# Batch 0 of an FFT convolution with an MLP behind it: stage A by pairs of columns, its output pushed into stage B's layout, the first D block kept on chip, weight conversions spread, tiles at multiples of 64 bytes

## The chip, the cores and the metric

One core of a Trainium2 chip runs the whole program. Its engines are TensorE (PE in the profile; PEld is its weight load), VectorE (DVE), ScalarE (ACT), GpSimd (POOL) and SyncE (SP), which here only issues transfers. The metric is the device time of one execution in microseconds; a comparison uses the median of several runs.

## What is computed

The input `x` is 8 batches of 3072 positions by 256 channels. Each channel is filtered along the positions in the frequency domain, and the result goes through a two-layer MLP with a softplus between.

```python
X = np.fft.rfft(x, axis=1)                       # (8, 3072, 256)
F = (filt_r + 1j * filt_i)[None, :, :]
y = np.fft.irfft(X * F, n=x.shape[1], axis=1)
h = y.reshape(-1, 256) @ w_in                    # 256 -> 2048
g = np.maximum(h, 0.0) + np.log1p(np.exp(-np.abs(h)))
out = g @ w_out                                  # 2048 -> 256
```

The weights arrive in float64 and are turned into float32 pairs on the chip.

## The kernel before

**Numbers.** Nearly every operand of a matmul is split into a rounded part and the rest (`hi_lo`, called `inh`/`inl`, `zh`/`zl`, `dih`/`dil`, `gh`/`gl` in the profile), and `split_mm` (line 67) makes three products of them. So each operand costs one cast and one subtraction before PE can use it.

**The transform** of 3072 = 128 x 12 x 2 positions goes in four stages per batch. *A*: for each of the 12 columns `i`, the two halves of `x` are added (even `i`) or subtracted (odd `i`), split, and multiplied by a 128x128 matrix `ca`; the output is `s1`. *B*: 13 units `u` of 120 rows (ten frequencies by twelve columns; the last has 96) are multiplied by `cb`; DVE multiplies the result with the filter rows `ft` in three instructions (lines 185, 186, 189), POOL adds the two halves (line 190). *C*: the inverse of B; the output `co` goes to DRAM as `s2`. *D*: for each of six blocks of 512 positions a last product, and the sums `y` that become the MLP's input `yT` (hi and lo).

Between A and B the layout changes: A's rows are frequencies, B's rows are (frequency, column). Later batches write A's output to DRAM and read it back in B's layout. Batch 0 keeps it on chip in `first_s1`, and each unit copies its part from ten partitions to 120 with two transfers on SP (line 153, `bi`), followed by two filter loads (lines 163 and 164, `ft`), through three rotating buffers each.

**The MLP** runs in 48 groups of 512 positions, 8 steps each. A step is `mm1` (12 products into `h`), ACT's Abs, Exp and Ln, then `soft` on DVE (the softplus row, line 298, the cast `gh`, line 300, the rest `gl`, line 302) and, two steps later, `mm2` (12 products into `o`). `h` has two buffers, so `mm1` of step s+2 waits for the softplus row of step s.

**Weights.** Each of 16 weight tiles is loaded with 512 KB (line 334) and converted by six DVE rows (`weight`, lines 348 to 361), then a cast on ACT and two POOL rows (`weight_ends`, lines 375 to 377). Tiles 0 to 7 belong to `w_in`: 2j and 2j+1 are needed by steps 2j and 2j+1. Tiles 8 to 15 belong to `w_out`: tile 8+s is needed by `mm2` of step s. `together` converts two tiles row by row in turn.

**What sets the order.** It is written by hand (`manual_schedule`): each engine executes its instructions in the order in which the Python code issues them. Batch 0 runs first, alone, through a table of visits (`first`); then the loop over steps interleaves the MLP of one batch with stages A to D of the next by a table of slots. Of the weights, 0, 1, 2 are converted in A and between A and B, 3 in the first unit of B, 8, 9, 4 between C and D, 5 and 11 behind D's first block, and the other seven one per step in `soft`:

```python
CONVERSIONS = {("a", 9): (0,), ("a", 11): (1, 2), ("b", 0): (3,), ("c", 12): (8, 9, 4)}
WEIGHTS = (5, 11), (10,), (6,), (7,), (12,), (13,), (14,), (15,)
```

An engine that waits holds all that is queued behind it. A transfer issued on SP or ACT also waits in that engine's order.

Of the kernel before, what the change touches and what calls it, by code (L numbers as in the profile page):

```python
# [25 lines left out]
F32 = mybir.dt.float32  # L26
# [8 lines left out]
NU = 13  # L35
# [3 lines left out]
LOADS = {("a", 8): (0,), ("a", 10): (2, 3), ("c", 9): (9,), ("c", 11): (8, 4), ("d", 1): (11,), ("y", 0): (5,)}  # L39
CONVERSIONS = {("a", 9): (0,), ("a", 11): (1, 2), ("b", 0): (3,), ("c", 12): (8, 9, 4)}  # L40
WEIGHTS = (5, 11), (10,), (6,), (7,), (12,), (13,), (14,), (15,)
TAGS = {1: "in", 2: "ca", 4: "in", 5: "in", 8: "in", 11: "ca"}
# [5 lines left out]
def fft_mlp(ctx: ExitStack, tc: tile.TileContext, x, fr, fi, ca, cb, cc, cd, w_in, w_out, out):  # L48
# [13 lines left out]
    wi = [const.tile([P, 2, FF], F32R, name=f"wi{k}") for k in range(2)]  # L62

# [19 lines left out]
    class Batch:  # L83
# [5 lines left out]
        def engines(self, first):  # L89

            return (nc.vector, nc.gpsimd) if self.b or first else (nc.scalar, nc.vector)

        def a_load(self, i):
            if i == 0 and self.b:
                self.s1 = dram.tile([2, P, N2, D], F32, tag="s1", name="s1")
            if self.b or i < 6:
                xt = work.tile([P, 2, 512], F32, tag="in", name="x", bufs=3)
            else:
                xt = start.tile([P, 2, 512], F32, name=f"x{i}")
# [4 lines left out]
            cat = (work if self.b or i >= 8 else start).tile(  # L104
                [P, 2, 2, 2, P], F32R, tag="ca" if self.b or i >= 8 else f"ca{i}", name="ca", bufs=2 if self.b or i >= 8 else 1
            )
# [11 lines left out]
        def a_prep(self, i):  # L118
            if self.b or i == 0:
                self.a_sum(i)  # L120
            st = self.t.pop(("as", i))
            if self.b == 0 and i + 1 < N2:
                self.a_sum(i + 1)
            self.t["ap", i] = hi_lo(st, P, "in", *self.engines(0))

        def a_mm(self, i):
# [7 lines left out]
            if self.b == 0:  # L134
                nc.scalar.activation(out=first_s1[i % 2][:, n2:n2 + 2].rearrange("p n d -> p (n d)"), in_=ps, func=AF.Copy)
                return
# [11 lines left out]
        def b_load(self, u):  # L148
            p = self.filled(u)
            bt = work.tile([P, 512], F32, tag="bi", name="bi", bufs=3)  # L150
            if self.b == 0:
                for h in range(2):
                    nc.sync.dma_start(
                        out=bt[:p, 256 * h:256 * h + 256],
                        in_=first_s1[h][10 * u:10 * u + p // N2],
                    )
# [308 lines left out]
    with tc.manual_schedule():  # L465
        nc.scalar.preload_act_table_set("natural_log_exp_and_others")
        def first(part):
            for q in part:
                p = seq[q][1:]
                run.ahead(q)  # L470
                if p == ("c", 2):
                    batches[0].e_load(0)
# [160 lines left out]
```

## Time and profile before

| what | value |
|---|---|
| runs | 2553.85, 2555.40, 2555.42 us; median 2555.4 |
| profiled execution | 2552.4 us, of which the span from first to last instruction is 2550.6 |
| mean granted TensorE clock | 0.975 |
| busy over the span | PE 2452.6 us (96%), DVE 2049.8 (80%), ACT 1494.8 (59%), POOL 747.3 (29%) |
| first product of A / of B / of D / of the MLP | 8.02 / 36.40 / 123.42 / 131.62 us |
| last copy of A begins; last row of C on ACT begins | 31.09; 113.72 us |
| softplus rows of steps 0 and 7 begin | 141.96 and 202.05 us |

All times are from the span's start. PE's share of 96% is an average: it is full for most of the program, and the places where it isn't are in the first 203 us. A busy time counts an instruction from its start to its end, and neighbours on one engine overlap a little, so for a chain of instructions the distance from start to start is the better price. What ended a wait stands in a row in brackets, or in the table of waits behind the arrow.

### The profile page before, as it was taken

The numbers are of one execution on the slowest core, as the hardware profiler recorded it, in microseconds if no ns is written. First come the engines' busy times: TensorE is split into PE (matmuls) and PEld (weight loads), VectorE is DVE, ScalarE is ACT, GpSimd is POOL, SyncE is SP. The second block draws the span as 40 slices with busy tenths as digits, with TensorE's granted clock in tenths as the row PEclk, the third lists the DMA queues.
The fourth block names the chain that finished last, engine by engine and source line by source line (L and its number), as shares of the span: only waits on it lengthen the run. The fifth ranks groups of instructions, "written<-read, shape, count | busy, mean of one in ns | idle before, by whom it ended". The sixth has DMA issues, their size and how long they took to land.

```text
span 2550.6 us, 31103 instructions
## 1 busy us (share of the span) xinstructions
PE 2452.6 (96%) x11232; PEld 2027.6 (79%) x11232; DVE 2049.8 (80%) x2575; ACT 1494.8 (59%) x1742; POOL 747.3 (29%) x610
## 2 busy tenths in 40 slices
PE   4589999999999999999999999999999999999999
PEld 3267777888888888888888888888888888888887
DVE  7799896889868898789878888688887899766665
ACT  3355655566656666666665666665665666665555
POOL 3544331333213332233313333143221433111110
PEclk7589999999999999999999999999999999999999
DMA  7724432343324341243323433233422533111100
GB/s 206 194 87 147 128 99 81 121 127 86 86 86 132 118 112 54 85 163 104 89 61 125 134 95 83 90 124 104 118 71 71 170 105 93 44 42 34 42 17 17
DMA packets 145673, 251.38 MB, mean 99 GB/s; under 512 B 12849, under 2 KB 63345, under 8 KB 145521
## 3 DMA queue, kind: packets, MB, share of 16 engines
q1 hardware_dynamic: 93168, 151.36, 19.4%
q0 software_dynamic: 14112, 50.86, 6.7%
q10 hardware_dynamic: 38240, 47.20, 6.3%
q8 instruction: 88, 1.44, 0.2%
q14 instruction: 65, 0.52, 0.1%
HBM read 173.87 MB, written 72.35 MB: 97 GB/s over the span
## 4 chain that ended last, share of the span: by engine, by line
PE 88%; DVE 6%; DMA 2%; issue 1%; ACT 1%; SPq 1%; POOL 0%; ACTq 0%; DVEq 0%; POOLq 0%
PE h L67 39%; PE o L67 39%; PE psd L245 3%; PE psa L67 2%; PE psb L67 2%; PE psc L67 2%; DMA bi<-s 1%; DVE s L298 1%; DMA x<-in_x 1%; DVE gl L302 0%; DVE gh L300 0%; DMA s<-co 0%; SPq L164 0%; DVE t L186 0%; DVE inh L73 0%
## 5 line engine op out<-in xcount | busy, mean ns | idle before, releaser
L67 PE MATMUL h<-yT,wi 128*128 128x512 f32 x4608 | 1117.9, 392 | 13.2 <-DVE s L298 11.6
L67 PEld LDWEIGHTS h<-yT,wi 128*128 128x128 f32 x4608 | 859.2, 189 | 190.1 <-DVE s L298 10.6
L67 PE MATMUL o<-gh,wo 128*128 128x512 f32 x3072 | 952.0, 391 | 5.6 <-ACT ob L325 5.2
L289 ACT ACTIVATE s<-h 128x1024 f32<-128x1024 f32 x384 | 395.0, 1029 | 717.1 <-PE h L67 678.3
L67 PEld LDWEIGHTS o<-gh,wo 128*128 128x128 f32 x3072 | 569.0, 189 | 118.1 <-ACT ob L325 5.9
L298 DVE SCALAR_TENSOR_TENSOR s<-h,s 128x1024 f32<-128x1024 f32 x384 | 467.9, 1219 | 178.2 <-ACT s L291 176.5
L67 PE MATMUL o<-gl,wo 128*128 128x512 f32 x1536 | 599.4, 390 | 3.7 <-DVE gl L302 3.7
L302 DVE TENSOR_TENSOR gl<-s,gh 128x1024 fp32r<-128x1024 f32 x384 | 471.4, 1228 | 36.5 <-DVE gh L300 0.9
L290 ACT ACTIVATE s<-s 128x1024 f32<-128x1024 f32 x384 | 407.8, 1062 | 12.2
L291 ACT ACTIVATE s<-s 128x1024 f32<-128x1024 f32 x384 | 407.7, 1062 | 12.2
L300 DVE CAST gh<-s 128x1024 fp32r<-128x1024 f32 x384 | 315.3, 821 | 36.6 <-DVE s L298 2.3
L67 PEld LDWEIGHTS o<-gl,wo 128*128 128x128 f32 x1536 | 289.0, 188 | 67.0 <-DVE gl L302 6.0
L271 POOL TENSOR_TENSOR yT<-y,yT 128x512 fp32r<-128x512 f32 x94 | 126.2, 1343 | 605.6 <-DVE yT L73 605.6
L190 POOL TENSOR_TENSOR t<-t,t 128x512 f32<-128x512 f32 x104 | 147.9, 1422 | 401.7 <-DVE t L189 295.5
L79 POOL TENSOR_TENSOR inl<-bi,inh 128x512 fp32r<-128x512 f32 (+2 forms) x100 | 132.4, 1324 | 293.3 <-issue 104.6
L79 POOL TENSOR_TENSOR dil<-di,dih 128x512 fp32r<-128x512 f32 x94 | 121.6, 1294 | 208.4 <-DVE dih L73 140.3
L257 DVE TENSOR_TENSOR sd<-psd,ev 128x256 f32<-128x256 f32 x192 | 80.6, 420 | 117.1 <-ACT ev L256 117.0
L79 POOL TENSOR_TENSOR inl<-st,inh 128x512 fp32r<-128x512 f32 x84 | 118.1, 1405 | 168.2 <-DVE inh L73 163.9
L79 DVE TENSOR_TENSOR zl<-t,zh 128x512 fp32r<-128x512 f32 x104 | 90.5, 870 | 56.3 <-ACT zh L71 54.0
L245 PE MATMUL psd<-cd,dih 128*128 128x256 f32 x384 | 100.9, 285 | 11.7 <-ACT dih L71 9.7
L245 PE MATMUL psd<-cd,dil 128*128 128x256 f32 x384 | 101.8, 286 | 3.0 <-DVE dil L79 3.0
L67 PE MATMUL psb<-inh,cb_sb 128*128 128x512 f32 (+3 forms) x224 | 73.0, 411 | 23.8 <-ACT inh L71 22.6
(60 smaller groups left out, 1806.9 us busy)
## 6 DMA issues: line engine op xcount, KB each, us to landing
ft<-in_fr SPq DMA_DIRECT2D x104, 256.0 KB
x<-in_x SPq DMA_DIRECT2D x48, 512.0 KB
ca<-in_ca POOLq DMA_DIRECT2D x48, 512.0 KB, 4.8
cd<-in_cd POOLq DMA_DIRECT2D x48, 512.0 KB, 4.0
di<-s SPq DMA_DIRECT2D x96, 256.0 KB
out<-ob SPq DMA_DIRECT2D x48, 512.0 KB
s<-co ACTq DMA_DIRECT2D x96, 240.0 KB
s<-ao ACTq DMA_DIRECT2D x84, 256.0 KB
```

Of the source, the lines that this page charges most:

```text
L67: nc.tensor.matmul(out=ps, lhsT=lhs[a], rhs=rhs[b], start=first and k == 0, stop=last and k == 2)
L79: lo_eng.tensor_sub(out=lo[:p], in0=src, in1=hi[:p].bitcast(F32))
L190: nc.gpsimd.tensor_add(out=t1, in0=t1, in1=t2)
L245: nc.tensor.matmul(out=ps[:, h].rearrange("p k n -> p (k n)"), lhsT=ds[k][:, h, 128 * c:128 * c + 128], rhs=cdt[:, h, j].rearrange("p k n ...
L257: nc.vector.tensor_add(out=s[:, j], in0=ps[:, :, 0], in1=ev)
L271: lo_eng.tensor_sub(out=lo[:, c], in0=y, in1=hi[:, c].bitcast(F32))
L289: nc.scalar.activation(out=a, in_=h, func=AF.Abs)
L290: nc.scalar.activation(out=a, in_=a, func=AF.Exp, scale=-1.0)
L291: nc.scalar.activation(out=a, in_=a, func=AF.Ln, bias=1.0)
L298: nc.vector.scalar_tensor_tensor(out=a, in0=h, scalar=0.0, in1=a, op0=ALU.max, op1=ALU.add)
L300: nc.vector.tensor_copy(out=hi, in_=a)
L302: nc.vector.tensor_sub(out=lo, in0=a, in1=hi.bitcast(F32))
```

## The change

Batch 0 gets code of its own, and the table of visits for it goes.

**A** (`first_a`) works by pairs of columns: one tile holds both halves' sum and difference, one ACT pass makes both casts, one DVE row both rests, 24 matmuls fill one two-bank accumulator, one ACT pass takes it out. The matrix `ca0` has its output columns reordered, so that a transfer can carry each column's rows straight into B's layout `s1b`: twelve pushes (`shuffle`), each of a 120-row and an 8-row transfer, alternately on SP and ACT. The pushes of pairs 0 and 1 are issued with pair 2.

**B and C** (`first_bc`) read `s1b` in place. All 26 filter loads are issued ahead on SP into tiles of their own, then the loads of weights 2, 8, 3, 4. Weights 0 and 1 are converted before B's first unit. The rests `inl` are made by DVE for units 0, 1, 2 and odd ones, else by POOL (before: by DVE for 0, 2, 3, 7). Each output of C, besides going to DRAM, is copied by two small transfers on SP into the first D block's input `di`, so D's load from DRAM falls away for that block.

**D** (`first_d`): weights 8 and 2 are converted before it, weight 3 in pieces between its rows. Weights 4 to 7 and 9 to 15 are left to the first eight steps, up to two per step. In those steps the cast `gh` is ACT's, and the second D block's casts are ACT's too. New pools lie at the right end of the memory, with each tile of theirs at a multiple of 64 bytes. The arithmetic is the same: PE has 10818 rows in either program, and from B's first unit on they are the same rows in the same order.

SP, where stages B and C of batch 0 end. Before (`s_82`, `s_83` are the two halves of A's output; `s_427` is `s2`):

```order
L153 DMA bi<-s_82 96x1x256
L153 DMA bi<-s_83 96x1x256
L163 DMA ft<-in_fr 128x512
L164 DMA ft<-in_fi 64x512
L334 DMA raw<-in_w_out 128x1024 x2
L334 DMA raw<-in_w_in 128x1024
L226 DMA di<-s_427 128x512 x2
```

and now (`raw` is a weight's tile):

```order
L466 DMA fr_315<-in_fr 128x512
L467 DMA fi_311<-in_fi 64x512
L466 DMA fr_319<-in_fr 128x512
L467 DMA fi_318<-in_fi 64x512
L327 DMA raw<-in_w_in 128x1024
L327 DMA raw<-in_w_out 128x1024
L327 DMA raw<-in_w_in 128x1024 x2
L203 DMA di<-co 10x2x256 x24
L203 DMA di<-co 8x2x256 x2
```

The copies `bi` are gone, the load of `di` from DRAM too, and the copies from `co` stand behind all filters and weights.

DVE, from stage A into B's first units. Now (`lo` is A's rest, lines 341 to 354 are a conversion, lines 170 to 174 the products with the filter):

```order
L520 TENSOR_TENSOR lo<-st,hi 128x1024 x2
L341 TENSOR_SCALAR m<-raw 128x512
L342 TENSOR_SCALAR p<-raw 128x512
L341 TENSOR_SCALAR m<-raw 128x512
L342 TENSOR_SCALAR p<-raw 128x512
L346 SCALAR_TENSOR_TENSOR raw<-raw,p 128x512 x2
L350 SCALAR_TENSOR_TENSOR raw<-m,raw 128x512 x2
L352 TENSOR_SCALAR p<-raw 128x512 x2
L354 SCALAR_TENSOR_TENSOR raw<-raw,p 128x512 x2
L79 TENSOR_TENSOR inl<-s1b,inh 120x512 x2
L170 TENSOR_TENSOR t_370<-psb,fr_273 128x512
```

Before, DVE's conversions of weights 0, 1 and 2 stood among A's last columns and behind them, and that of weight 3 behind the products of B's first unit; now both conversions stand between A's last row and B's first.

DVE, from the softplus row of one early step to the next. Before:

```order
L298 SCALAR_TENSOR_TENSOR s<-h,s 128x1024
L348 TENSOR_SCALAR m<-raw 128x512
L349 TENSOR_SCALAR p<-raw 128x512
L300 CAST gh<-s 128x1024
L353 SCALAR_TENSOR_TENSOR raw<-raw,p 128x512
L302 TENSOR_TENSOR gl<-s,gh 128x1024
L357 SCALAR_TENSOR_TENSOR raw<-m,raw 128x512
L359 TENSOR_SCALAR p<-raw 128x512
L361 SCALAR_TENSOR_TENSOR raw<-raw,p 128x512
```

and now, in the step with weights 5 and 9:

```order
L291 SCALAR_TENSOR_TENSOR s<-h,s 128x1024
L341 TENSOR_SCALAR m<-raw 128x512
L342 TENSOR_SCALAR p<-raw 128x512
L346 SCALAR_TENSOR_TENSOR raw<-raw,p 128x512
L295 TENSOR_TENSOR gl<-s,gh 128x1024
L350 SCALAR_TENSOR_TENSOR raw<-m,raw 128x512
L352 TENSOR_SCALAR p<-raw 128x512
L354 SCALAR_TENSOR_TENSOR raw<-raw,p 128x512
L341 TENSOR_SCALAR m<-raw 128x512
L342 TENSOR_SCALAR p<-raw 128x512
L346 SCALAR_TENSOR_TENSOR raw<-raw,p 128x512
L350 SCALAR_TENSOR_TENSOR raw<-m,raw 128x512
```

The cast `gh` has left DVE, and a second conversion stands behind the first.

The core of the diff:

```diff
+WEIGHTS = (4,), (5, 9), (10, 6), (7, 11), (12,), (13,), (14,), (15,)
...
-        def engines(self, first):
-            return (nc.vector, nc.gpsimd) if self.b or first else (nc.scalar, nc.vector)
+        def engines(self, blk):
+            if self.b or blk > 1:
+                return nc.vector, nc.gpsimd
+            return nc.scalar, nc.gpsimd if blk else nc.vector
...
-            if self.b == 0:
-                for h in range(2):
-                    nc.sync.dma_start(
-                        out=bt[:p, 256 * h:256 * h + 256],
-                        in_=first_s1[h][10 * u:10 * u + p // N2],
-                    )
...
-            self.t["bp", u] = hi_lo(self.t["b", u][0][:p], p, "in", hi_eng, lo_eng if u in (0, 2, 3, 7) else nc.gpsimd)
+            self.t["bp", u] = hi_lo(src[:p], p, "in", hi_eng, lo_eng if u < 3 or u % 2 else nc.gpsimd)
...
+            if self.b == 0:
+                dt = self.t["d", 0][0]
+                for n in range(2):
+                    nc.sync.dma_start(
+                        out=dt[10 * u:10 * u + p // N2, :, n],
+                        in_=co[:p].rearrange("(r n) (h d) -> n r h d", n=N2, h=2)[n],
+                    )
...
-        nc.vector.tensor_copy(out=hi, in_=a)
+        copy(nc.scalar if s < len(WEIGHTS) else nc.vector, hi, a)
...
+    def filter_load(v, pool):
+        fit = pool.tile([P, 512], F32, name=f"fi{v}", align_bytes=64)
...
+            nc.sync.dma_start(out=frt, in_=fr[u])
+            nc.sync.dma_start(out=half, in_=fi[u])
...
+    def first_a(s1_b, start):
...
+        def sums(p):
+            xt = xts.pop(p)
+            st = sts[p] = start.tile([P, 2, 512], F32, tag="st", name="st", align_bytes=64)
+            nc.vector.tensor_add(out=st[:, 0], in0=xt[:, 0], in1=xt[:, 1])
+            nc.vector.tensor_sub(out=st[:, 1], in0=xt[:, 0], in1=xt[:, 1])
+            his[p] = start.tile([P, 2, 512], F32R, tag="hi", name="hi", align_bytes=64)
+            nc.scalar.activation(out=his[p], in_=st, func=AF.Copy)
+
+        def shuffle(p):
+            ao = aos.pop(p)
+            for j in range(2):
+                eng = (nc.sync, nc.scalar)[j]
+                for q, rows, u in ((slice(0, 120), 120, slice(0, NU - 1)), (slice(120, P), 96, slice(NU - 1, NU))):
+                    eng.dma_start(
+                        out=s1_b[:rows, u].rearrange("(r n) u c -> n r u c", n=N2)[2 * p + j],
+                        in_=ao[q, j],
+                    )
...
+            if p >= 2:
+                shuffle(p)
+            if 3 <= p < 5:
+                weight_load(p - 3)
+
+    def first_bc(s1_b, filters, pool):
...
+        for k in (2, 8, 3, 4):
+            weight_load(k)
+        together((0, 1))
+        weight_ends()
+        bt.e_load(0)
+        bt.t["d", 0] = work.tile([P, 2, 2, D], F32, tag="di", name="di"), bt.t.pop(("e", 0))
+        bt.b_prep(0)
+        for i in range(NU + 2):
+            if i + 1 < NU:
+                bt.b_prep(i + 1)
+            if i < NU:
+                bt.b_mm(i)
+            if 0 < i <= NU:
+                bt.z_mm(i - 1)
+            if i >= 2:
+                bt.c_mm(i - 2)
...
+    def first_d():
+        together((8, 2))
+        weight_ends()
+        more = weight(3)
+        bt.d_prep(0)
+        bt.d_prep(1)
+        for _, k, i in d_visits(0):
+            getattr(bt, f"{k}_mm")(i)
+            next(more, None)
...
-                soft(s, chain(*(weight(k) for k in (WEIGHTS[s + 1] if s + 1 < len(WEIGHTS) else ()))))
+                soft(s, chain(*(weight(k) for k in (WEIGHTS[s] if s < len(WEIGHTS) else ()))))
...
+    order = [10 * u + r for r in range(10) for u in range(NU - 1)] + list(range(120, 128))
```

More of the change, by code (lines that the diff above doesn't have):

```diff
@@ L62, in fft_mlp @@
     wi = [const.tile([P, 2, FF], F32R, name=f"wi{k}") for k in range(2)]
+    other = dict(side="right", reuse_waits="tile")
     def split_mm(ps, lhs, rhs, first=True, last=True):
@@ L465, in fft_mlp @@
+    def first_d():
[7 more added lines that the diff above has]
+            next(more, None)
+        for _ in more:
+            pass
+        weight_ends()
     with tc.manual_schedule():
         nc.scalar.preload_act_table_set("natural_log_exp_and_others")
[L467 to L472, printed above, removed]
-                run.do(q)
-                for k in LOADS.get(p, ()):
-                    weight_load(k)
-                together(CONVERSIONS.get(p, ()))
-                weight_ends()
@@ L479, in fft_mlp @@
-        seq = visits(batches[0], "a") + visits(batches[0], "b") + d_visits(0)
-        run = Run([[p] for p in seq], 2)
-        b_end = seq.index((batches[0], "b", NU - 1)) + 1
-        with tc.tile_pool(name="first", bufs=1) as first_pool:
-            first_s1 = [first_pool.tile([P, N2, D], F32, name=f"s1{h}") for h in range(2)]
-            with tc.tile_pool(name="start", bufs=1) as start:
-                for i in range(NP):
-                    if i == NP - 1:
-                        weight_load(1)
-                    batches[0].a_load(2 * i)
-                nc.gpsimd.dma_start(out=cb_sb, in_=cb)
-                nc.gpsimd.dma_start(out=cc_sb, in_=cc)
-                run.classes[0]["load"] = NP
-                first(range(N2))
-            first(range(N2, b_end))
@@ L495, in fft_mlp @@
-        late = ctx.enter_context(tc.tile_pool(name="late", bufs=1))
-        wo = [late.tile([P, 16, D], F32R, name=f"wo{k}") for k in range(2)]
-        mlp = ctx.enter_context(tc.tile_pool(name="mlp", bufs=2))
-        first(range(b_end, len(seq)))
-        together(WEIGHTS[0])
+        bt = batches[0]
+        with tc.tile_pool(name="first", bufs=1, **other) as first_pool:
+            s1_b = first_pool.tile([P, NU, 512], F32, name="s1b", align_bytes=64)
+            with tc.tile_pool(name="start", bufs=2, **other) as start:
+                first_a(s1_b, start)
+                filters = filter_load(0, first_pool)
+            with tc.tile_pool(name="filter", bufs=1, **other) as pool:
+                first_bc(s1_b, filters, pool)
@@ L501, in fft_mlp @@
+        late = ctx.enter_context(tc.tile_pool(name="late", bufs=1, **other))
+        wo = [late.tile([P, 16, D], F32R, name=f"wo{k}", align_bytes=64) for k in range(2)]
+        mlp = ctx.enter_context(tc.tile_pool(name="mlp", bufs=2, **other))
+        first_d()
         for k in WEIGHTS[1]:
```

106 lines of the change are left out of this document (71 added, 35 removed).

## The prediction

> **What bounds the kernel now.** I read the table of stretches first, cut at the events the change touches (columns: stretch, length, then busy time and instruction count of PE, PEld, DVE, ACT and POOL, granted clock, DMA share, GB/s).
>
> ```profile
> 0.00:32.00 32.00, 15.13 (x72) 12.02 (x72) 22.25 (x35) 15.55 (x26) 7.52 (x14) 0.91 0.81 282
> 32.00:114.00 82.00, 45.92 (x84) 22.49 (x84) 58.38 (x75) 24.34 (x42) 39.47 (x29) 0.50 0.67 161
> 114.00:142.00 28.00, 13.75 (x40) 9.87 (x40) 24.46 (x41) 9.11 (x16) 11.72 (x8) 0.55 0.43 138
> 142.00:203.30 61.30, 46.47 (x184) 34.95 (x184) 60.57 (x79) 31.21 (x37) 30.68 (x25) 0.94 0.28 95
> 203.30:2550.60 2347.30, 2331.37 (x10852) 1948.25 (x10852) 1884.11 (x2349) 1414.59 (x1623) 657.96 (x535) 1.00 0.31 93
> ```
>
> From 203.3 us on PE is busy 99% at the full clock. From there the engines' rows stand in the same order in both programs, apart from what one step still finishes, so I leave those 2347.3 us alone. What can move is the first 203.3 us: batch 0, and then a stretch in which DVE is busy 60.57 of 61.30 us while PE waits.
>
> The 82 us from 32 to 114 hold stages B and C of batch 0. No engine is full there and the clock is half. Their largest wait, SP's rows for one unit, and SP's rows for the same filters in a later batch:
>
> ```profile
> ACT inh L71 <- DMA bi<-s: 37.1, 11, 4.6
> 54.77 1.64 SPq L153 DMA_DIRECT2D bi<-s  x2
> 56.51 1.42 SPq L163 DMA_DIRECT2D ft<-in_fr  x1
> 57.98 2.58 SPq L164 DMA_DIRECT2D ft<-in_fi  x1
> 288.96 0.34 SPq L163 DMA_DIRECT2D ft<-in_fr  x1
> 289.36 0.47 SPq L164 DMA_DIRECT2D ft<-in_fi  x1
> ```
>
> ACT waits 37.1 us for `bi`, the copy of A's output into B's layout. SP spends 1.64+1.42+2.58 = 5.64 us per unit issuing four transfers, and a unit takes 82/13 = 6.3 us; the two filter loads alone cost 0.34+0.47 = 0.81 us when their queue is free. A queue of transfers, not an engine, sets B and C.
>
> **The change part by part.** *A by pairs, pushed.* The rows that price it:
>
> ```profile
> 22.01 0.69 DVE L116 TENSOR_TENSOR st<-x 128x512 f32<-128x512 f32 x1 [1.26 <-DMA x<-in_x]
> 31.09 0.60 ACT L135 ACTIVATE s<-psa 128x512 f32<-128x512 f32 x1 [2.49 <-PE psa L67]
> 36.40 0.80 PE L67 MATMUL psb<-inh,cb_sb 120*128 120x256 f32 x2 [5.36 <-ACT inh L71]
> L302 DVE TENSOR_TENSOR gl<-s,gh 128x1024 fp32r<-128x1024 f32 x384 | 471.4, 1228 | 36.5 <-DVE gh L300 0.9
> L290 ACT ACTIVATE s<-s 128x1024 f32<-128x1024 f32 x384 | 407.8, 1062 | 12.2
> 207.92 0.71 PE psa L67 x6
> q1 hardware_dynamic: 5232, 6.93, 55.5%
> ```
>
> The last `x` was used at 22.0, A's last copy ended at 31.7, B's first product stood at 36.4. The new A loads the same bytes at a DMA share that was 0.81, so its last tile again lands at about 22. Behind it come two sums on DVE (0.69 each), one 1024-wide pass on ACT (1.06), one 1024-wide difference on DVE (1.23), 24 products (4 x 0.71), ACT's copy (1.06) and ACT's issue of the push, for which I take 0.8, half of SP's row for two copies from ten partitions: 8.4. With 1.5 for ACT still being at the pair before, A ends at 32. The pushes are 12 x 128 packets of 2 KB. The row of queue 1 (40 to 100 us; packets, MB, share of 16 engines) prices a packet, over on-chip copies and loads, at 0.555 x 16 x 60 / 5232 = 0.102 us, so they take 1536 x 0.102 / 16 = 10 us of all engines, beside the loads. Five of SP's six pushes stand ahead of weight 1 on its queue; I let that weight land at 35.
>
> *Weights 0 and 1 ahead of B.* DVE converts them before its first B row, and waits for weight 1 with every `inl` and product behind it:
>
> ```profile
> 112.62 0.42 DVE L348 TENSOR_SCALAR m<-raw 128x512 uint32<-128x512 uint32 x1
> 118.25 0.42 DVE L348 TENSOR_SCALAR m<-raw 128x512 uint32<-128x512 uint32 x1
> ```
>
> Interleaved, two weights take 118.25-112.62 = 5.6 us. So E, the time at which DVE may begin B, is 35+6 = 41. Bounds: 37, where only the conversion follows A's last difference, and 51, from the late pushes below.
>
> *B and C.* `bi` is gone and the filters are queued ahead, so the engines set the unit:
>
> ```profile
> 74.80 0.69 DVE L79 TENSOR_TENSOR inl<-bi,inh 120x512 fp32r<-120x512 f32 x1 [2.14 <-ACT inh L71]
> 75.41 0.68 DVE L185 TENSOR_TENSOR t<-psb,ft 128x512 f32<-128x512 f32 x1
> 77.53 0.69 DVE L79 TENSOR_TENSOR zl<-t,zh 128x512 fp32r<-128x512 f32 x1
> 78.31 0.69 DVE L185 TENSOR_TENSOR t<-psb,ft 128x512 f32<-128x512 f32 x1
> 79.02 0.69 DVE L186 SCALAR_TENSOR_TENSOR t<-psb,ft 64x512 f32<-64x512 f32 x1
> 79.72 0.68 DVE L189 TENSOR_TENSOR t<-psb,ft 64x512 f32<-64x512 f32 x1
> 59.85 1.05 PE L67 MATMUL psb<-inh,cb_sb 120*128 120x512 f32 x2
> 60.70 0.63 PE L67 MATMUL psb<-inl,cb_sb 120*128 120x512 f32 x1
> 63.29 0.63 ACT L71 ACTIVATE inh<-bi 120x512 fp32r<-120x512 f32 x1 [4.42 <-PE psc L67]
> 64.43 0.32 ACTq L210 DMA_DIRECT2D s<-co  x1
> 82.33 1.28 POOL L190 TENSOR_TENSOR t<-t,t 128x512 f32<-128x512 f32 x1
> 82.57 1.58 DVE L79 TENSOR_TENSOR zl<-t,zh 128x512 fp32r<-128x512 f32 x1 [2.16 <-ACT zh L71]
> 116.93 3.22 POOL L376 TENSOR_TENSOR raw<-raw,wo 128x512 f32<-128x512 f32 x1 [6.83 <-DVE p L359]
> ```
>
> From start to start, three DVE products and `zl` take 0.71+0.70+0.70+0.78 = 2.9 us, and `inl` 0.61 in 8 of 13 units: 3.25 on average. Beneath that lie PE's six matmuls (0.85 for two, so 2.6 even at half clock), ACT's three passes and a store (3 x 0.63+0.32 = 2.2) and POOL's one or two adds of 1.28. DVE and POOL can block each other: the `zl` at 82.57 took 1.58 and ended after POOL's add of 82.33. But POOL's row at 116.93 took 3.22 while DVE ran independent rows without a gap, so an `inl` right behind `zl` should keep POOL out. I add 0.2, about half of `zl`'s 0.9 excess every second unit: 3.45, bounds 3.25 and 4.3 (a POOL add in most units). The first unit takes 5.3 (two `inl` of 1.6, like `zl` at 82.57, beside POOL's weight rows, then the products), twelve more 41.4, the drain through POOL, ACT and `zl` 3.3: DVE ends B and C at E+50 = 91.
>
> The Trainium skill speaks against this at one place. "SBUF — State Buffer", section Who interferes with whom, says that a DVE instruction with two SBUF inputs and a POOL instruction that reads SBUF exclude each other for the whole instruction, and that the order of issue decides. The row at 82.57 agrees; if POOL's add is issued before `inl`, the sum is the lock rival's below.
>
> *First D block on chip.* Its load from DRAM goes; 26 small copies out of `co` come, on SP's queue behind 26 filter and 4 weight loads. At 0.81 us per filter pair SP is past the filters at 32+11 = 43; by the packet price their 2496 packets need 16 us, so at 50 or so with the weights. The first `co` is ready near 54. I take no wait; bounds 0 and 28 (a rival). The last copy lands under the conversion that follows; without that cover it would cost some 2 us.
>
> *Conversions, D, and the loop's start.*
>
> ```profile
> 124.95 3.22 DVE L79 TENSOR_TENSOR dil<-di,dih 128x512 fp32r<-128x512 f32 x2
> 141.96 1.23 DVE L298 SCALAR_TENSOR_TENSOR s<-h,s 128x1024 f32<-128x1024 f32 x1 [0.85 <-ACT s L291]
> 151.34 1.53 DVE L73 CAST dih<-di 128x512 fp32r<-128x512 f32 x1
> 168.20 1.27 DVE L349 TENSOR_SCALAR p<-raw 128x512 uint32<-128x512 uint32 x1
> 178.41 0.43 DVE L349 TENSOR_SCALAR p<-raw 128x512 uint32<-128x512 uint32 x1
> 178.76 0.67 DVE L300 CAST gh<-s 128x1024 fp32r<-128x1024 f32 x1
> 202.05 1.21 DVE L298 SCALAR_TENSOR_TENSOR s<-h,s 128x1024 f32<-128x1024 f32 x1
> ```
>
> Three weights stood between C and D, now two do, 5.6 us: 96.6. The two `dil` beside POOL's weight rows take 3.2 again: 99.8. From their end at 128.2 to the first softplus row on DVE (141.96) it is 13.8 us; weight 3's rows, threaded into D, add 2 of their 2.8 (bounds 0 and 2.8). First softplus: 115.6, 26 us earlier. In that latency the old kernel converted weights 5 and 11; the new one leaves it empty, so more is left for the loop.
>
> From the first softplus row to the eighth DVE needed 202.05-141.96 = 60.1 us, with seven conversions; now ten lie there. A conversion is 2.8 and up to 0.85 that one of its rows loses beside POOL (1.27 against 0.43): 3 x 3.65 = +11. Seven `gh` casts go to ACT (-4.7), and a contended `dih` (-1.5). ACT's new round, `gh`, three 1.06 passes and then DVE's 1.2, is 5.4 us against DVE's 6 or more, so it hides; uncovered it would cost half a microsecond a step. Net +5, rounded up to 6 for it; bounds 0 and 10. The 64-byte rule costs nothing: these tiles are whole multiples of 1 KB, and in both programs all begin at multiples of 64 bytes.
>
> **Sum.** 26-6 = 20. The profiled execution, 2552.4 (1.8 outside its span), becomes 2532.4. The median of the runs stands 3.0 above that execution: 2535.4, said as 2535.
>
> **The rivals.** *Lock.* POOL's add gets in between `zl` and `inl`: eight waits of 1.28, 10 us, 2545. For it the row of 1.58, against it that of 3.22. Chance 0.15.
>
> *Late pushes.* If the pushes, 3.1 MB, only run at the 161 GB/s of the stretch that held B's on-chip copies, they take 20 us; with 2.5 MB of loads still to come at the first stretch's 282 GB/s, 9 us, they end at 17+29 = 46, weight 1 with them: E = 51, and 2545. For it: such copies were what ACT waited for. Against: those read ten neighbouring partitions, these write partitions twelve apart. Chance 0.12. The Trainium skill, "DMA: Bandwidth & Descriptors", section Why a DMA increments its semaphore by 16 and not by 1, lets a transfer use as many engines as divide the outer sizes of both sides, ten here; by it the 10 us of pushes would be about 15. No row here counts engines.
>
> *SP's queue, the slower side.* SP issues in order. If a filter pair costs what it did in stage B (1.42+2.58 = 4.0) and not 0.81, SP reaches the first `co` copy at 32+13 x 4.0+2 = 86. Two `co` buffers hold ACT meanwhile, with `inh` and `zh` queued behind, and DVE behind those, from about 60 to 88: 28 us, 2563. It decides from some 3.7 us per pair. Against it: those pairs stood behind `bi`, which is gone. Chance 0.07.
>
> *Nothing moves.* DVE's work is only shifted, and the loop gives all back: 2555. Against: DVE idled 82-58.4 = 24 us in B and C, which this fills. Chance 0.08.
>
> **How the numbers follow.** My case has 0.55, with 2527 to 2542 as its own range (E 37 to 45, unit 3.25 to 3.8, loop 2 to 9); a larger gain has 0.03. The range, 2526 to 2551, leaves out the slower and most of the even case. About 0.2%, 5 us, is what a measurement of this kernel tells from no change: faster 0.83, same 0.09, slower 0.08.
>
> **What would show it.** A's last copy ends near 32, DVE begins B between 38 and 45, its products recur every 3.3 to 3.7 us with no wait for `bi`, filters or `co`; first softplus near 116, eighth near 182, PE unbroken from there. B starting after 50, units over 4 us, ACT held by `co` for tens of us, or over 72 us between those softplus rows would each name the failed step, and a change in the stretch behind 203 us would make the whole sum wrong.

## The result, and the profile after

The changed kernel is slower: 2598.07 us (median of four runs, 2596.51 to 2599.58) against 2554.62 for the kernel before beside it (2551.50 to 2555.42). The ratio is 1.0172, 95% interval 1.0155 to 1.019. The prediction, 2535 in a range of 2526 to 2551 and faster with 0.83, was wrong in sign. The profiled execution of the changed kernel took 2599.58 us, its span 2597.6.

Most of the loss is not in the stretch that the change was written for. This is the chain of work in order of time at 1200 us, deep in the steady part (start, length, what; `h` is the first product's output, `o` the second's; the short groups of stages B to D between them are left out). First the kernel before:

```profile
1202.79 2.72 PE h L67 x12
1205.51 2.72 PE o L67 x12
1208.71 2.75 PE h L67 x12
1212.13 2.72 PE o L67 x12
```

and the changed one:

```profile
1200.40 2.77 PE h L67 x12
1203.86 2.79 PE o L67 x12
1207.35 2.77 PE h L67 x12
1210.58 2.80 PE o L67 x12
```

With those short groups, both chains are TensorE alone, with no gap. But the same twelve products take 2.77 to 2.80 us where they took 2.72 to 2.75. The table of stretches (columns as in the prediction) shows it as fewer products in the same time. Before:

```profile
400.00:1000.00 600.00, 599.95 (x2809) 502.53 (x2808) 495.63 (x623) 367.13 (x425) 181.45 (x148) 1.00 0.34 103
1000.00:1500.00 500.00, 500.00 (x2357) 419.38 (x2356) 407.74 (x513) 304.34 (x351) 151.09 (x124) 1.00 0.35 107
```

and after:

```profile
400.00:1000.00 600.00, 600.00 (x2764) 493.90 (x2763) 487.18 (x615) 360.32 (x418) 177.85 (x146) 1.00 0.34 101
1000.00:1500.00 500.00, 500.00 (x2319) 412.17 (x2318) 399.46 (x501) 300.36 (x346) 148.16 (x122) 1.00 0.33 103
```

PE is busy throughout and its granted clock is 1.00 in all four rows, yet it gets through 1.6% fewer products. "PE busy 100%" did not mean "at its best pace".

The head gained nothing either. The softplus rows of the twelfth step before, and of the first, eighth and twelfth now:

```profile
225.18 1.21 DVE L298 SCALAR_TENSOR_TENSOR s<-h,s 128x1024 f32<-128x1024 f32 x1
```

```profile
133.45 1.23 DVE L291 SCALAR_TENSOR_TENSOR s<-h,s 128x1024 f32<-128x1024 f32 x1 [6.81 <-ACT s L284]
204.25 1.21 DVE L291 SCALAR_TENSOR_TENSOR s<-h,s 128x1024 f32<-128x1024 f32 x1
233.77 1.21 DVE L291 SCALAR_TENSOR_TENSOR s<-h,s 128x1024 f32<-128x1024 f32 x1
```

The first row comes 8.5 us earlier than before (141.96), the eighth 2.2 later (202.05), the twelfth 8.6 later. From the twelfth row to the end of the span it is 2597.6-233.77 = 2363.8 us, against 2550.6-225.18 = 2325.4. So the 47.0 us between these two spans (the medians, 43.5 apart, lie a little nearer) are 8.6 from the head and 38.4 from a stretch that executes the same instructions in the same order: from the twelfth row on, the two traces hold the same rows on every engine, 10749 products among them. (Over the whole span either trace holds 11232 products, where the text ahead of the prediction names 10818 rows.)

The rows of the head that answer to the prediction's steps, on ACT, DVE and SP:

```profile
23.94 1.02 ACT L532 ACTIVATE ao<-psa 128x1024 f32<-128x1024 f32 x1 [6.41 <-DMA s1b<-ao]
34.44 1.02 ACT L532 ACTIVATE ao<-psa 128x1024 f32<-128x1024 f32 x1 [1.72 <-PE psa L67]
42.83 0.43 DVE L341 TENSOR_SCALAR m<-raw 128x512 uint32<-128x512 uint32 x1 [6.24 <-DMA raw<-in_w_in]
47.79 1.29 DVE L79 TENSOR_TENSOR inl<-s1b,inh 120x512 fp32r<-120x512 f32 x2
69.43 2.63 SPq L203 DMA_DIRECT2D di<-co  x3
```

A's last copy began at 34.4, after ACT had waited 6.41 us for the pushes to give `ao` buffers back. Weight 1 landed only at 42.8, and DVE began B at 47.8. SP reached the first `di` copy at 69.4. The table of waits (us in total, times, longest us) says what that cost from 36 to 112 us, in the first two rows, and what held PE in the loop's first steps from 133 to 206 us, in the third:

```profile
DVE zl L79 <- ACT zh L71: 11.3, 3, 8.1
ACT co L194 <- DMA di<-co: 10.7, 1, 10.7
PE o L67 <- ACT wo L368: 14.8, 2, 7.9
```

### The profile page after: what moved, and what is told of

It reads as the page before. It is cut to its first block, busy times and chain, and to the rows that moved or that the text cites. A ratio compares the mean times of both kernels' runs of the same rounds, so it can differ in the third digit from the quotient of the medians.

```text
span 2597.6 us, 31070 instructions
## 1 busy us (share of the span) xinstructions
PE 2491.1 (96%) x11232; PEld 2033.0 (78%) x11232; DVE 2039.2 (79%) x2561; ACT 1504.8 (58%) x1742; POOL 745.3 (29%) x606
## 4 chain that ended last, share of the span: by engine, by line
PE 89%; DVE 5%; ACT 1%; issue 1%; POOL 0%; DVEq 0%; POOLq 0%; ACTq 0%
PE o L67 39%; PE h L67 39%; PE psd L238 3%; PE psb L67 2%; PE psa L67 2%; PE psc L67 2%; DVE s L291 1%; DVE p L342 0%; DVE gl L295 0%; DVE m L341 0%; ACT s L282 0%; DVE gh L73 0%; ACT s L283 0%; DVE inh L73 0%; DVE raw L346 0%
## 5 line engine op out<-in xcount | busy, mean ns | idle before, releaser
L67 PE MATMUL h<-yT,wi 128*128 128x512 f32 x4608 | 1130.2, 393 | 5.4 <-ACT yT L71 3.8
L67 PE MATMUL o<-gh,wo 128*128 128x512 f32 x3072 | 974.9, 398 | 31.9 <-ACT wo L368 14.8
L67 PE MATMUL o<-gl,wo 128*128 128x512 f32 x1536 | 611.7, 398 | 0.6 <-DVE gl L295 0.6
L73 DVE CAST gh<-s 128x1024 fp32r<-128x1024 f32 x376 | 305.7, 813 | 35.4 <-DVE s L291 0.5
L79 POOL TENSOR_TENSOR inl<-bi,inh 128x512 fp32r<-128x512 f32 (+1 forms) x91 | 120.9, 1329 | 279.5 <-issue 113.6
L79 DVE TENSOR_TENSOR zl<-t,zh 128x512 fp32r<-128x512 f32 x104 | 84.3, 810 | 57.8 <-ACT zh L71 55.3
L238 PE MATMUL psd<-cd,dil 128*128 128x256 f32 x384 | 100.3, 283 | 0.7 <-DVE dil L79 0.7
L71 ACT ACTIVATE zh<-t 128x512 fp32r<-128x512 f32 x104 | 65.0, 625 | 59.0 <-POOL t L175 55.2
```

The source lines that it names most:

```text
L67: nc.tensor.matmul(out=ps, lhsT=lhs[a], rhs=rhs[b], start=first and k == 0, stop=last and k == 2)
L73: eng.tensor_copy(out=out, in_=in_)
L79: lo_eng.tensor_sub(out=lo[:p], in0=src, in1=hi[:p].bitcast(F32))
L238: nc.tensor.matmul(out=ps[:, h].rearrange("p k n -> p (k n)"), lhsT=ds[k][:, h, 128 * c:128 * c + 128], rhs=cdt[:, h, j].rearrange("p k n ...
```

## The experiments

Two questions: why TensorE's products got slower behind 206 us, and what ate the head's gain.

**Where the tiles lie.** The instructions behind the head are the same, so I looked at addresses. In the kernel before, every tile begins 128 bytes behind a whole 1024 in each partition. In the changed one `wi` still does, but the tiles of the new right-hand pools don't: `yT` hi and lo begin 768 and 832 bytes behind a whole 1024, `wo` 960, `gh` and `gl` 896 (the numbers with which the replay below repeats this kernel). So `wo` and half of `yT` begin at odd multiples of 64. My first theory was that such an address is slow. Four kernels tried it. For all kernels of this section the pace is given as the mean time of twelve products, from the start of the first to the start of the row behind them, over some 320 groups of either product between 400 and 2400 us of the trace (the few with a stop of some 0.1 us or more left out).

*after_128.*

```diff
-align_bytes=64
+align_bytes=128        # everywhere
```

> The changed kernel with one number changed: every tile that the change puts at a multiple of 64 bytes stands at a multiple of 128 bytes (wo, yT, s, gh, gl and the first batch's tiles; the instructions and their order stay). In the changed kernel wo0, wo1, yT1 and s begin at an odd multiple of 64 bytes, in the kernel before every tile begins at a multiple of 128. Theory ADDRESS (TensorE takes longer over operands that begin at an odd multiple of 64): products of 128x512 come every 226.5 to 227 ns behind 210 us as before, against 230.9 (first product) and 233 (second) now, 384 steps get 108 ns each back, and the time is 2598 - 42 = about 2556 us. Theory PLACE (the tiles' other place or order in the memory, their right-hand end among it, or which tiles share a bank): nothing changes, 2598. Theory OTHER (something in the program that is no address, as the first batch's leftovers): nothing changes, 2598.

*before_all64.* One unused tile ahead of `wo`.

```diff
+        late.tile([P, 16], F32, name="pad0")
         wo = [late.tile([P, 16, D], F32R, name=f"wo{k}") for k in range(2)]
```

> The kernel before with one unused tile of 64 bytes ahead of wo: wo, yT, s, gh and gl stand 64 bytes further on, all at odd multiples of 64, and nothing else changes. ADDRESS: the steady stretch loses what the changed kernel loses or more, since yT0, gh and gl are off now too: 42 us or more, 2597 to 2640 us. PLACE and OTHER: 2555, no change.

*before_wo64.* The same, and a second one behind `wo`.

```diff
+        late.tile([P, 16], F32, name="pad0")
         wo = [late.tile([P, 16, D], F32R, name=f"wo{k}") for k in range(2)]
+        late.tile([P, 16], F32, name="pad1")
```

> The kernel before with 64 unused bytes ahead of wo and 64 behind it: only wo, the fixed operand of the second product, stands at an odd multiple of 64; yT, gh and gl at multiples of 128. ADDRESS by the fixed operand: the second product comes every 233 ns, the first every 226.5 to 227, 4608 products x 6 ns = about 28 us, 2583 us. ADDRESS by the moving operand alone: no change, 2555. PLACE and OTHER: 2555.

*before_mlp64.* Only the second one.

> The kernel before with 64 unused bytes behind wo: wo stands where it stood, and yT, s, gh and gl, the moving operands and the softplus's tile, at odd multiples of 64. ADDRESS by the moving operand: both products slower, 4 to 6 ns each, 9216 x 4 to 6 = 37 to 55 us, 2592 to 2610 us. ADDRESS by the fixed operand alone: no change, 2555. PLACE and OTHER: 2555.

Measured: after_128 2601.8 us (1.0192, 1.0177 to 1.0208), before_all64 2573.2 (1.0075, 1.0058 to 1.0092), before_wo64 2584.8 (1.0124, 1.0104 to 1.0145), before_mlp64 2595.8 (1.0168, 1.0147 to 1.0188), against 2553.3 for the kernel before. The theory of odd multiples of 64 falls at once with after_128, which has none and is no quicker. But 64 or 128 unused bytes in the old kernel, which change no instruction, cost 20 to 43 us. So placement it is, and the time is TensorE's; the chains of before_mlp64 and of after_128 at 1200 us:

```profile
1206.39 2.76 PE o L67 x12
1209.15 2.75 PE h L67 x12
1219.06 2.81 PE o L67 x12
```

```profile
1210.74 2.80 PE o L67 x12
1213.54 2.80 PE h L67 x12
```

before_wo64 has a correction to its expectation: its two pads moved `yT`, `gh` and `gl` too, by 128. So the nearness of its 2584.8 to the 2583 that the theory gave for a slow fixed operand is luck: the first product, which doesn't read `wo`, lost more (2788 ns for twelve against 2730) than the second (2762). What the four share with the changed kernel is that the fixed tile and the moving tile of at least one of the two products no longer have the same remainder by 512. In before_all64 the second product, with `wo`, `gh` and `gl` all moved by 64, kept nearly its pace (2744 ns for twelve against 2730), and the first, with `yT` moved against `wi`, lost (2772). That made the next theory: the distance between the two operands of a product counts, not where either lies.

*after_res128.* All alignments out, and one unused tile at the right end, so that the right-hand tiles also begin 128 behind a whole 1024.

```diff
-align_bytes=64         # everywhere
+        edge = ctx.enter_context(tc.tile_pool(name="edge", bufs=1, **other))
+        edge.tile([P, 216], F32, name="pad")
         with tc.tile_pool(name="first", bufs=1, **other) as first_pool:
```

> The changed kernel with its 64-byte rule taken out and one unused tile of 864 bytes at the right-hand end instead, so that wo, yT, s, gh and gl all begin 128 bytes behind a whole 1024, as wi and every tile of the kernel before do; the instructions and their order stay. What the four runs before leave: no product is quick or slow by its own address (wo moved alone by 64 slowed the first product too, which does not read it), but in the kernel before the fixed and the moving tile of each product have the same remainder by 512, and where they do not, the products are slower. Theory RELATION (the distance of the fixed tile from the moving one, by its remainder, sets the pace): both products back at 226.5 to 227 ns, 2598 - 42 = about 2556 us, or about 2 more for what the head lost. Theory PLACE (the right-hand side of the memory itself): 2598, unchanged.

*before_allshift.*

```diff
+    const.tile([P, 16], F32, name="pad")
     cb_sb = const.tile([P, 2, 2, P], F32R, name="cb_sb")
```

> The kernel before with one unused tile of 64 bytes ahead of its first constant: all tiles, wi and the working tiles too, begin 192 bytes behind a whole 1024, at odd multiples of 64, and their distances stay. RELATION: no change, 2553 to 2556 us, 226.5 to 227 ns for both products. Rival ABSOLUTE (a tile at an odd multiple of 64 costs whatever reads it): 20 to 45 us slower, 2573 to 2600.

after_res128 took 2560.64 us, 1.0027 (1.0016 to 1.0037): 37.4 us of the 43.5 came back through an unused tile and the alignments taken out. So PLACE, the right-hand side itself, falls. before_allshift took 2554.16, 1.0003 (0.9994 to 1.0013): every tile at an odd multiple of 64, and nothing lost. Both have 2731 ns for twelve of either product. The chain of after_res128 at 1200 us is that of the kernel before again, while its twelfth softplus row (the second fence) stays where the changed kernel had it:

```profile
1201.54 2.72 PE o L67 x12
1204.73 2.75 PE h L67 x12
1211.38 2.72 PE h L67 x12
```

```profile
233.76 1.21 DVE L291 SCALAR_TENSOR_TENSOR s<-h,s 128x1024 f32<-128x1024 f32 x1
```

So the two losses are apart: placement 37 us, the head 7.

*pace.* The disputed cost by itself:

```diff
+    def look(name, n, still_at, moving_at, beside=None):
+        for k in range(n):
...
+            a = 256 * (k % 16) + still_at[k % len(still_at)] // 4
+            b = 512 * (k // 3 % 10) + moving_at[k % len(moving_at)] // 4
+            nc.tensor.matmul(out=p, lhsT=still[:, a:a + 128], rhs=moving[:, b:b + 512], start=k % 6 == 0, stop=k % 6 == 5)
...
+        for m in range(0, 1024, 64):
+            look(f"m{m}x", 60, (0,), (m,))
```

> Not the kernel's work: 60 products of 128x512 with a new fixed tile each, for each of 41 placements, on an otherwise idle core (the last of them with copies on VectorE beside); the output is no result. Names: m64x is the moving tile 64 bytes on and the fixed one at a whole 1024, s64x the fixed one 64 bytes on, both64x both, mix64x every third moving tile 64 on, dve64x both in place with VectorE's copy 64 on. RELATION: m0x, m512x, s512x and all both rows at 226.5 ns; m64x to m448x, s64x to s256x at 229 to 234 ns; mix rows between. ABSOLUTE: m64x, m192x, s64x, both64x, both192x slower, m128x, m256x as m0x. Rival OTHER ENGINES (TensorE is slowed by what the other engines read and write at that remainder): all rows without VectorE at one pace, the dve rows apart.

The groups of instructions by name (count, then busy time, mean ns of one, idle time before them). A group's busy time is 59 distances and one product's own 0.39 us, so 13.8 stands for 227 ns, 13.9 for 229, 14.1 for 232 and 14.2 for 234 a product. The distance is how far the moving tile's address lies behind the fixed one's.

```profile
L67 PE MATMUL m0x<-moving,still 128*128 128x512 f32 x60 | 13.8, 389 | 0.0
L67 PE MATMUL m64x<-moving,still 128*128 128x512 f32 x60 | 13.9, 392 | 0.0
L67 PE MATMUL m128x<-moving,still 128*128 128x512 f32 x60 | 14.1, 395 | 0.0
L67 PE MATMUL m192x<-moving,still 128*128 128x512 f32 x60 | 14.2, 394 | 0.0
L67 PE MATMUL m256x<-moving,still 128*128 128x512 f32 x60 | 13.8, 389 | 0.0
L67 PE MATMUL m320x<-moving,still 128*128 128x512 f32 x60 | 13.9, 392 | 0.0
L67 PE MATMUL m32x<-moving,still 128*128 128x512 f32 x60 | 14.2, 395 | 0.0
L67 PE MATMUL s64x<-moving,still 128*128 128x512 f32 x60 | 14.2, 394 | 0.0
L67 PE MATMUL both64x<-moving,still 128*128 128x512 f32 x60 | 13.8, 389 | 0.0
L67 PE MATMUL dve64x<-moving,still 128*128 128x512 f32 x60 | 13.8, 389 | 0.0
```

From start to start the means are 226.7 ns at distance 0, 229.2 at 64, 232.5 at 128, 233.3 at 192, 227.0 at 256, 229.2 at 320, and so on round to 960: the period is 256 bytes. Moving the fixed tile on by 64 (233.3) is the same as moving the other one by 192. Moving both together costs nothing (227.1), and VectorE copying beside it costs nothing (226.7). Distances that aren't multiples of 64 were slow too (32: 233.3, 4: 237.7). RELATION holds, with 256 in place of the 512 that I had written; ABSOLUTE and OTHER ENGINES fall.

*replay.* One row doesn't settle the kernels, since their triples mix distances: after_128 has the hi tiles at distance 0 and the lo tiles at 128.

```diff
+        for n in range(12):
+            o, m, (a, b) = n // 6, n // 3 % 2, ((0, 0), (1, 0), (0, 1))[n % 3]
+            f = fixed[a] // 4 + (step * i + inner[0] * o + inner[1] * m) // 4
+            g = moved[b] // 4 + 512 * m
...
+            steps("A", 10, 128, (128, 128), 128, (128, 128))
+            steps("B", 10, 128, (768, 832), 960, (896, 896))
```

> Not the kernel's work: groups of twelve products in the kernel's own order (h as the first product, o as the second, in turn) with the remainders by 1024 at which six of the kernels hold wi, yT, wo, gh and gl, on a core where nothing but TensorE works; the output is no result. A is the kernel before, B the changed one, C after_128, D before_all64, E before_wo64, F before_mlp64, G before_allshift. The single row of distances (0: 226.7 ns, 64: 229.2, 128: 232.5, 192: 233.3, period 256) does not give all of the kernels' paces: after_128 runs its products at 232 though two of three are at distance 0. If TensorE's own reads, in their order, are all of it, the groups of twelve repeat the kernels within 6 ns: A 2730 and 2730 ns, B 2772 and 2796, C 2787 and 2785, D 2772 and 2744, E 2788 and 2762, F 2782 and 2784, G 2730. If the other engines' traffic has a share, the groups are nearer to 2730 than the kernels' are.

| kernel | distance by 256, first / second product (hi, lo where they differ) | twelve products in the kernel, ns | in the replay, ns |
|---|---|---|---|
| before | 0 / 0 | 2730, 2730 | 2721, 2720 |
| after | 128, 192 / 192 | 2772, 2796 | 2773, 2786 |
| after_128 | 0, 128 / 0, 128 | 2787, 2785 | 2773, 2773 |
| before_all64 | 64 / 0 | 2772, 2744 | 2749, 2720 |
| before_wo64 | 128 / 64 | 2788, 2762 | 2793, 2757 |
| before_mlp64 | 64 / 64 | 2782, 2784 | 2746, 2747 |
| before_allshift | 0 / 0 | 2731, 2731 | 2721, 2720 |

The replay's rows of the kernel before (A) and of the changed one (B), 240 products each:

```profile
L64 PE MATMUL hA<-moving,still 128*128 128x512 f32 x240 | 57.7, 389 | 0.0
L64 PE MATMUL oA<-moving,still 128*128 128x512 f32 x240 | 57.6, 389 | 0.0
L64 PE MATMUL hB<-moving,still 128*128 128x512 f32 x240 | 58.7, 393 | 0.0
L64 PE MATMUL oB<-moving,still 128*128 128x512 f32 x240 | 59.0, 394 | 0.0
```

With only TensorE at work every group that has products at an uneven distance is slow and every group at distance 0 is quick. For the changed kernel the replay gives 53 and 66 ns more than at distance 0, the kernel itself 42 and 66. So TensorE's own work is enough for its loss. "Within 6 ns" fell, though: the kernels have some 10 ns more even at distance 0, and at distance 64 before_mlp64 loses twice what the replay loses (52 and 54 against 26 and 27), while the second product of before_wo64 loses about as much (32 against 37).

The kernels' traces show where the rest stands. In the kernel before, each of the 254 groups that directly follow another group of `h` or `o` takes 2720 ns, as in the replay; nearly all behind a product of stage A or D take some 27 ns more. In before_mlp64 a group takes either 2746 to 2764 ns (248 groups) or 2798 to 2803 (385), and each of the 244 that directly follow another group of `h` or `o` keeps the pace of the one ahead. So the rest goes with what TensorE did just before, which the replay leaves out; a share of the other engines' traffic isn't needed for it. That is read from the traces; no run put the stages' products into the replay, and none shows why a pace carries on.

The Trainium skill, "SBUF — State Buffer", section Who interferes with whom, gives TensorE two read ports, one for the moving operand and one for the weight load, calls them independent, and knows one kind of contention only, that of VectorE and GpSimd. These runs disagree: the same products go from 226.7 to 233.3 ns on a core where nothing else works, by the distance of those two operands alone. Whether it is the reads themselves or something ahead of them that conflicts, no run here shows.

**What ate the head's gain.** Three kernels mend one part of the head each, on after_res128 so that placement is out of it, and one mends all. The diffs leave out what after_res128 has already.

*r_copies.* Eight units' filters stay ahead of B; the other filters and the four weights are asked for between the units.

```diff
-            if u not in filters:
+            if u not in filters and u < 8:
                 filters.update(filter_load(u // 2, pool))
-        for k in (2, 8, 3, 4):
-            weight_load(k)
...
                 bt.c_mm(i - 2)
+            if i in (2, 4, 6):
+                filters.update(filter_load(i // 2 + 3, pool))
+            for k in {7: (2,), 8: (8,), 9: (3,), 10: (4,)}.get(i, ()):
+                weight_load(k)
```

> The changed kernel with the mended places (after_res128, 2560.6 us), and one edit in its head: only the first eight units' filters are asked for ahead of B, the other five and weights 2, 8, 3 and 4 between the units, behind the copies into di, so that these don't stand behind 24 transfers on SP's queue. Theory QUEUE (the head's loss in B and C is that queue): ScalarE's wait for di<-co falls from 11.4 us to under 3, VectorE's for zl from 8.8 to under 2, the first softplus moves from 133.6 to about 126, and the end by as much: about 2553 us. Rival RAMP (the eight steps behind are bound by VectorE and by late weights whatever comes before, so a head that ends sooner only waits there): first softplus at 126, the twelfth at 232 to 234 as now, 2559 to 2561. Rival LANDING (the copies are late by the transfers' own time, not by their place in the queue): no row moves by over 2 us, 2560.

*r_pairs.* Two edits at once: other buffers for pairs 2 and 3, and weights 0 and 1 asked for one pair earlier.

```diff
-            ao = aos[p] = work.tile([P, 2, 512], F32, tag="ob", name="ao")
+            ao = aos[p] = work.tile([P, 2, 512], F32, tag=("ob", "di", "ob")[p // 2], name="ao")
-            if 3 <= p < 5:
-                weight_load(p - 3)
...
                 sums(p + 1)
+            if 2 <= p < 4:
+                weight_load(p - 2)
```

> The mended changed kernel and one edit in stage A: the output of pairs 2 and 3 goes to the two idle di buffers instead of waiting for the ob buffers that pairs 0 and 1 are still being pushed from, and weights 0 and 1 are asked for one pair earlier, ahead of that pair's push. ScalarE's wait for DMA s1b<-ao (6.6 us) and VectorE's two waits for raw (9.1 us) should go, B should begin at about 40 us instead of 47.5, the first softplus come at 126 instead of 133.6, and the time be 2553 to 2555 us if the rest follows (theory SUM); 2559 to 2561 if the ramp swallows it (RAMP); if the transfers are the bound there (their engines are 0.8 to 0.9 busy until 28 us), B begins no earlier than 45 and the time is 2558 to 2560.

*r_weights.*

```diff
-WEIGHTS = (4,), (5, 9), (10, 6), (7, 11), (12,), (13,), (14,), (15,)
+WEIGHTS = (9,), (5,), (10,), (11, 6), (12, 7), (13,), (14,), (15,)
...
-        together((8, 2))
+        together((8,))
...
         weight_ends()
+        together((2, 4))
...
-        for k in WEIGHTS[1]:
+        for k in WEIGHTS[0] + WEIGHTS[1]:
             weight_load(k)
```

> The mended changed kernel and one edit in the conversions: only weight 8 ahead of D, weights 2 and 4 behind D in VectorE's hole ahead of the first softplus (3.6 and 3.2 us idle there), and the other nine spread as 9 / 5 / 10 / 11 and 6 / 12 and 7 / 13 / 14 / 15 over the first eight steps, where the changed kernel had 4 / 5 and 9 / 10 and 6 / 7 and 11 / 12 / 13 / 14 / 15. Theory RAMP (the steps with two conversions cost 11.6 to 15.5 us where one with one costs 5.5 to 10; VectorE is busy throughout there): first softplus at 131 to 135, the eighth at 197 to 200 instead of 204.3, the time 2554 to 2556 us. Rival ORDER (TensorE's order, with second products waiting for late weights, sets it, and these are no earlier): 2559 to 2562.

*r_all.* The edits of r_copies, r_pairs and r_weights together.

> All three edits of the head on the mended changed kernel. SUM (each gain passes to the end): 2560.6 less 7.5, 7 and 5 = about 2541 us, first softplus at 117 to 119. RAMP or the transfers swallow a part: 2546 to 2553. No gain: 2560.

| kernel | us | ratio to before, 95% | first / twelfth softplus row, us |
|---|---|---|---|
| before | 2552.94 to 2553.24 | 1 | 141.96 / 225.18 |
| after_res128 | 2560.64 | 1.0027 (1.0016 to 1.0037) | 133.56 / 233.76 |
| r_copies | 2550.07 | 0.9989 (0.998 to 0.9998) | 123.84 / 224.02 |
| r_pairs | 2555.50 | 1.0010 (1.0001 to 1.0019) | 128.18 / 229.95 |
| r_weights | 2558.31 | 1.0021 (1.0012 to 1.003) | 133.56 / 232.30 |
| r_all | 2543.31 | 0.9961 (0.9948 to 0.9973) | 116.18 / 214.15 |

r_copies gained 10.6 us, more than the 7.5 expected, and its twelfth row moved by 9.7: QUEUE holds, LANDING and RAMP fall. SP's first copy goes out at 58.96 now:

```profile
58.96 1.76 SPq L203 DMA_DIRECT2D di<-co  x2
63.33 5.64 SPq L203 DMA_DIRECT2D di<-co  x4
```

r_pairs gained 5.1 us, but not as expected. A's last copy came no earlier (35.6 us): ACT stood 5.9 us a step later, a wait that the profile puts down to the same pushes. What moved is weight 1, and with it B's start, which then waited for filters:

```profile
33.57 0.42 DVE L341 TENSOR_SCALAR m<-raw 128x512 uint32<-128x512 uint32 x1
42.48 2.32 DVE L79 TENSOR_TENSOR inl<-s1b,inh 120x512 fp32r<-120x512 f32 x2 [3.87 <-DMA fr<-in_fr]
```

r_weights gained 2.3 of the 5 expected. From the first softplus row to the twelfth it still needs 98.7 us, against 100.2 in after_res128 and 83.2 in the kernel before: spreading the conversions differently hardly helps. Its eighth row came at 201.26 us (204.32 in after_res128) where RAMP expected 197 to 200, and its 2558.3 us lies between what RAMP and ORDER gave, so this run settles neither.

r_all gained 17.3 us on after_res128 against 18.0 for the three single gains added, so the gains pass to the end nearly whole. At 2543.3 us it beats both kernels, the one before by 0.39% (0.27 to 0.52). Its first row comes at 116.18 and its twelfth at 214.15, 11.0 us ahead of the kernel before:

```profile
116.18 1.21 DVE L291 SCALAR_TENSOR_TENSOR s<-h,s 128x1024 f32<-128x1024 f32 x1
214.15 1.21 DVE L291 SCALAR_TENSOR_TENSOR s<-h,s 128x1024 f32<-128x1024 f32 x1
```

## Why the prediction was wrong, step by step

**The step that failed** is the sentence "The 64-byte rule costs nothing: these tiles are whole multiples of 1 KB, and in both programs all begin at multiples of 64 bytes", and with it "I leave those 2347.3 us alone". The order of the rows was the same, as I said; I took that for the same time. In place of 0 the term measured 37.4 us (after against after_res128), and 38.4 between the twelfth softplus row and the end of the two traces. I had looked at each address by itself where the distance between a product's two operands was what counted. That a change behind 203 us would make the whole sum wrong stood in the prediction, but no chance was given to it, and none of the four rivals holds it. Had the placement been that of after_res128, the time would have been 2560.6, still outside the range: the head failed too.

**A ends at 32.** 34.4+1.0 = 35.5. The wait that I left out is ACT's 6.41 us for `ao` buffers, because the pushes of pairs 0 and 1 are issued late and hold both. With buffers given (r_pairs) ACT waited for the pushes in another place and A ended no earlier, so the lack of buffers alone does not set A's end; what does was not settled.

**Weight 1 lands at 35, E = 41.** It landed at 42.8 and E was 47.8, within my bounds (37 and 51). Asked for one pair earlier, it is converted from 33.6 and B begins at 42.5.

**The unit, 3.45 us.** Undisturbed it was 3.7: two units take 7.3 us at 91 us in the trace. The lock between VectorE and GpSimd is in it, but small. Of the six `inl` that VectorE made from the third unit on, four ran beside POOL's add and took 1.25 to 1.67 us where the one at 57.58 took 0.68, about 3 us in all against the 10 of the rival *Lock*:

```profile
87.13 1.72 POOL L175 TENSOR_TENSOR t<-t,t 128x512 f32<-128x512 f32 x1
88.15 1.25 DVE L79 TENSOR_TENSOR inl<-s1b,inh 120x512 fp32r<-120x512 f32 x1 [0.43 <-ACT inh L71]
```

This `inl` waited for ACT's `inh`, so it did not stand right behind `zl`, as I had assumed, and the add was under way.

**SP's queue, no wait taken.** I put 28 us at the far bound and gave it 0.07. ACT was held 10.7 us, and the edit that frees it is worth 10.6. The mechanism of that rival was right, its size was between: SP was past the filters neither at 43 nor at 86, but issued its first copy at 69.4. It began the filters at 40.98, where I had taken 32, because of the pushes ahead of them. Its filter rows did not cost 4.0 us per pair: most took 0.5 each, and the rest of the loss is one stand of 7 us with shorter ones after it, for which the packet price, 50 us or so, made no room:

```profile
55.69 0.33 SPq L466 DMA_DIRECT2D fr<-in_fr  x1
62.66 0.47 SPq L467 DMA_DIRECT2D fi<-in_fi  x1
```

That SP stood there because the queue was full is inferred, not tried.

**First softplus 115.6.** It came at 133.45. E (6.8) and the queue (some 10) explain 17 of the 18: in r_copies, which has no such wait, it is 123.84-47.2 = 76.6 us from E to that row, against the predicted 115.6-41 = 74.6. The middle of the sum was nearly right, in part by luck: in r_copies the two `dil` took 1.3 us where I counted 3.2, and from their end to the softplus it was 18.6 where I counted 15.8.

**The ramp, +6.** From the first to the eighth row it is 70.8 us against 60.1: +10.7, just beyond my upper bound of 10. And it doesn't end there. To the twelfth row it is 100.3 against 83.2: +17.1. I had counted ten conversions against seven up to the eighth row; the eleventh lies behind it, in what I called "what one step still finishes". Four conversions at my 3.65 are 14.6. The savings that I set against them, 4.7 for `gh` on ACT and 1.5 for `dih`, don't show in the sum; neither was tried alone. In r_all the ramp is still 98.0 us.

**The rivals.** *Late pushes* gave E 51 where my case gave 41; it was 47.8. Whether the pushes' bandwidth or weight 1's place on SP's queue made it late, no run separates. *Nothing moves* is nearest for the head (after_res128 is 0.27% slower than before), but not as it said: the work was not only shifted. The waits and the ramp took the gain, and with the three edits of r_all the head is worth 9.6 us.

## What to carry to other kernels

An unchanged order of instructions is not an unchanged time: when a change moves tiles, compare TensorE's pace in the steady part (products per stretch, or twelve products in the chain of waits) even where PE is 100% busy in both. For products like these, put the fixed and the moving tile at the same remainder by 256 bytes; here one unused tile, with the 64-byte alignment taken out, did it and was worth 37 us. And when small transfers that an engine waits for are put on a queue, put them ahead of bulk that isn't needed yet, and count work that is moved into a saturated stretch to the end of that stretch.

## What the runs showed of the hardware that I had not expected

A 128x512 product of fp32r with a new fixed tile each time takes 226.7 ns when the two operands' addresses differ by a multiple of 256 bytes, and 229.2, 232.5 or 233.3 ns at 64, 128 or 192 bytes more, with single products up to 241; at 4 bytes the mean is 237.7. The absolute address doesn't matter (all tiles moved by 64: 1.0003). Products with different distances disturb each other: a row of two at distance 0 and one at 64 takes 231.8 ns each, where the rows of either distance by itself would average 227.5; two at 0 and one at 128 take 229.0 in a plain row, but 231.1 in the kernel's order of hi and lo (2773/12). And a pace can carry on: in before_mlp64 each of the 244 groups that directly follow another of `h` or `o` keeps that group's pace, 2746 or 2800 ns for twelve.
